# Causal conv and gated FFN on one core: the opening's taps, bands, x cast and first transposes rearranged

## The chip, the cores and the metric

The kernel runs on one core of a Trainium2 chip. The metric is the device time of one execution in microseconds; the time before is the median of three runs. Engines are named as in the profile: PE is TensorE (its weight loads are PEld), DVE is VectorE, ACT is ScalarE, POOL is GpSimd, SP is SyncE, which here issues most transfers.

## The reference

Two stages. First a causal depthwise conv: x is 8 x 4096 x 192, the 192 channels fall into 8 heads of 24, and each head has 7 taps, the softmax of its row of `weight`. Then, on the 32768 x 192 result, a feed-forward stage with 2048 hidden values and the activation h cos(h).

```
w   = softmax(weight, axis=-1)                  # (8, 7)
out[b, s, h, :] = sum_k w[h, k] * x_pad[b, s + k, h, :]    # 6 zero rows ahead of each sequence
h   = out.reshape(32768, 192) @ w_in            # (192, 2048)
y   = (h * cos(h)) @ w_out                      # (2048, 192), float32
```

## The kernel before

**Tiling.** The tokens go in 64 tiles of 512, two to a unit of 1024. For each tile the hidden values come in 8 steps of 256: PE multiplies by w_in into a PSUM tile `h` (`mm1`, L503, a ring of three), ACT takes the cosine (L510), DVE multiplies h by it (L514), and PE multiplies the product by w_out into `o_ps` (`mm2_step`, L552). The conv of later units is made beside this work.

**The conv as a matmul.** A conv over 128 tokens is a matmul with a banded matrix: `band` holds for each head a 128 x 256 matrix, the first half for the tokens' own block and the second for the block behind them. A band consists of four blocks of 32 rows by 38 columns that are alike (E = 38 = 32 + 6). The kernel builds one such block per head and copies it into place. Heads are kept on quarters of the partitions: partitions 32q to 32q + 31 hold the two heads 2q and 2q + 1 (HQ = 2).

**The opening, in program order.** All order is by hand: each engine works off its instructions in the order in which the program gives them.

- ACT issues the load of `weight` into `w_row`, four partitions of 14 values (L81); SP issues the load of the first four blocks of x (L102).
- PE runs zero matmuls that keep its clock up (`keep_warm`, L136). POOL makes `quarter` (L140 to L143), a 4 x 128 matrix of ones in four runs of 32, and one fp32 matmul (L150) spreads the taps to the partitions: `w_bc` is 128 x 14.
- POOL makes `mask` (L158, L159), 32 x 38 x 7, one where tap k of row p falls on column e; ACT and DVE copy it to the other three quarters (L164). POOL then issues the load of w_in (L112), clears a block, and makes the identity (L170).
- Softmax of the taps: maximum and difference on DVE (L176, L178), exponential on ACT (L179), which then loads the table of the sine (L180); sum, reciprocal and product on DVE (L182 to L185) give `wn` in bf16.
- ACT casts the first four blocks of x to bf16 (L398, at L219 in the profile).
- DVE multiplies mask by wn into `prod` (L401, bf16) and sums over the taps into `diag` (L404), 128 x 2 x 38. Behind this sum SP may issue the further loads of x (L406 to L410).
- 16 copies put diag into band (L415): the letters of a string give the engine of each, D for DVE, P for POOL, A for ACT.
- `conv_first` (L426): 32 matmuls in two halves of two blocks each. The result has 64 channels in each of three chunks per block, and each copy (ACT for the first half, DVE for the second, L438) writes them twice side by side into `ct`, since the product with w_in wants every channel on both halves of the partitions. Behind the second copy SP issues the four loads of w_out (L124).
- `turn_first` (L445): for each block three transposes on PE against the identity, 128 columns of ct (a chunk twice) at a time (L453), copied into `cT` by ACT or DVE (L457). Two zero matmuls (one in the second half) stand ahead of them. Then the first tile's products start.

Two strings per tile (`PE_ORDER`, `PE_FIRST`, `ACT_ORDER`, `ACT_FIRST`) give the order of the rest: `h` is a step of mm1, `m` so many steps of mm2, `W` the cast of half of w_out on POOL (L120), `r`, `c`, `d` parts of later convs, `s` a cosine and its product, `p` and `q` marks that the mm2 steps of a tile or half a tile are done.

Of the kernel before, what the change touches and what calls it, by code (L numbers as in the profile page):

```python
# [8 lines left out]
FP32 = mybir.dt.float32  # L9
# [7 lines left out]
def kernel(  # L17
# [8 lines left out]
    nc = tc.nc  # L26
# [52 lines left out]
    HQ = H // 4  # L79
    w_row = consts.tile([4, HQ * K], FP32)  # L80
    nc.scalar.dma_start(out=w_row, in_=weight.rearrange("(q h) k -> q (h k)", q=4))  # L81

# [44 lines left out]

    one = consts.tile([128, 1], FP32)
    nc.vector.memset(one, 1.0)
# [4 lines left out]
    def keep_warm(n, bank=idle):  # L134
        for _ in range(n):
            nc.tensor.matmul(out=bank, lhsT=zero[:, 0:128], rhs=zero, start=True, stop=True)  # L136


    quarter = consts.tile([4, 128], FP32)
    nc.gpsimd.memset(quarter, 1.0)  # L140
    nc.gpsimd.affine_select(out=quarter, in_=quarter, compare_op=ALU.is_ge, fill=0.0, base=0, pattern=[[1, 128]],
                            channel_multiplier=-32)
    nc.gpsimd.affine_select(out=quarter, in_=quarter, compare_op=ALU.is_ge, fill=0.0, base=31, pattern=[[-1, 128]],  # L143
                            channel_multiplier=32)
    scrap = consts.tile([128, 1], FP32)
    nc.scalar.activation(out=scrap, in_=one, func=AF.Exp)
# [3 lines left out]
    nc.tensor.matmul(out=w_all[:, 0 : HQ * K], lhsT=quarter, rhs=w_row, start=True, stop=True)  # L150
    keep_warm(9)

# [25 lines left out]
    nc.vector.tensor_tensor(out=wexp, in0=w_bc, in1=wmax.to_broadcast([128, HQ, K]), op=ALU.subtract)  # L178
    nc.scalar.activation(out=wexp, in_=wexp, func=AF.Exp)  # L179
    nc.scalar.activation(out=scrap, in_=one, func=AF.Sin)  # L180
    wsum = consts.tile([128, HQ, 1], FP32)
    nc.vector.tensor_reduce(out=wsum[:, :, 0], in_=wexp, axis=mybir.AxisListType.X, op=ALU.add)  # L182
# [169 lines left out]
    def taps(u, j, half, mul):  # L352
        if u not in pa:
            pa[u] = pa_pool.tile([128, PA, WN, OR], FP32, name="pa")
        part = slice(HALF * half, HALF * (half + 1))
        mul(pa[u][:, j, part], tap_window(u, j)[:, part], tap[:, j : j + 1])  # L356
# [3 lines left out]
    def conv_raw(u):  # L360

        a, p = pa.pop(u), raw_prod
# [26 lines left out]
    def mend_edges(u):  # L389
# [7 lines left out]

    cast_unit(0, 0, NB, nc.scalar.copy)  # L398

    prod = consts.tile([128, HQ, E, K], BF16)  # L400
    nc.vector.tensor_tensor(out=prod, in0=mask.rearrange("p (o e) k -> p o e k", o=1).to_broadcast([128, HQ, E, K]),  # L401
                            in1=wn.rearrange("p h (o k) -> p h o k", o=1).to_broadcast([128, HQ, E, K]), op=ALU.mult)
    diag = consts.tile([128, HQ, E], FP32)
    summed = nc.vector.tensor_reduce(out=diag, in_=prod, axis=mybir.AxisListType.X, op=ALU.add)  # L404

# [13 lines left out]
    for i in range(2):  # L419
        nc.gpsimd.affine_select(out=pick[:, i, :, :, i, :], in_=pick[:, i, :, :, i, :], compare_op=ALU.not_equal, fill=1.0,  # L420
                                base=0, pattern=[[0, 2], [-32, 4], [0, R]], channel_multiplier=1)
    ct_tiles[0] = ct_pool.tile([128, UB + 1, NC, 2, 64], BF16, name="ct")
    cT[0] = cT_pool.tile([128, NC * (UB + 1) * 128], BF16, name="cT")
    copies = [nc.scalar.copy, nc.vector.tensor_copy]

    def conv_first():  # L426

        banks = o_banks()
        for half in range(2):
            for h in range(H):  # L430
                for prev in range(2):
# [5 lines left out]
                        start=(h == 0 and prev == 0), stop=(h == H - 1 and prev == 1), skip_group_check=True)  # L437
            m = copies[half](out=ct_tiles[0][:, 2 * half : 2 * half + 2].rearrange("p n k t w -> p (n k) t w"),  # L438
                             in_=banks[half][:, 0 : 2 * D].rearrange("p (m t w) -> p m t w", t=1, w=64).to_broadcast(
                                 [128, 2 * NC, 2, 64]))  # L440
        tc.add_manual_dep(nc.sync.nop().ins, m.ins.name, sync_dep, reason="order of the transfers")
# [3 lines left out]
    def turn_first(half):  # L445
        for n in range(2):
# [5 lines left out]
            for k in range(NC):  # L452
                nc.tensor.matmul(out=ps[:, k * 128 : (k + 1) * 128],  # L453
                                 lhsT=ct_tiles[0][:, 2 * half + n, k, :, :].rearrange("p t w -> p (t w)"), rhs=ident,
                                 start=True, stop=True, skip_group_check=True)
            m = NC * (2 * half + n)
# [131 lines left out]

    PE_ORDER = ['m12 h0 m4 h1 K+3 R+1 m5 h2 m7 q h3 U+0 m6 h4 m17 h5 X+1 m9 p h6 h7 O m4', 'm11 h0 m4 h1 m6 h2 m7 q x+1 h3 m5 h4 m7 c1 m8 c2 m3 h5 T+3 L+4 m9 p O h6 h7 m4']
    ACT_ORDER = ['s0 s1 a211 s2 s3 s4 a014 a114 Q s5 P s6 s7 a007', 's0 s1 s2 a102 s3 a203 s4 Q ec2 ec1 s5 P s6 s7']  # L590

    PE_FIRST = ["K1 h0a h0b W0 h1 h2 h3 r h4 w5 d11 w4 h5 d21 W1 c11 X0 m1 h6 m11 h7 L2 c21 D1",
# [5 lines left out]
    ACT_FIRST = ["s0a s0b s1 s2 er s3 s4 ed11 ed21 s5 ec11 s6 ec21 s7",  # L598
                "s0 s1 s2 s3 s4 s5 ec12 ec22 Q P s6 ed12 s7 ed22 ec13 ec23",
                "s0 s1 s2 s3 Q s4 P s5 s6 s7",  # L600
                "s0 s1 s2 s3 s4 ed13 ed23 Q s5 P s6 s7"] + ACT_ORDER

    PE_LAST = "m10 h0 m3 h1 m13 h2 m2 q h3 m10 h4 m3 h5 m7 h6 m12 p h7 O m7"
    ACT_LAST = "s0 s1 s2 s3 s4 s5 s6 P A s7"
# [7 lines left out]
    for t in range(NT + 1):  # L612
        u, second = divmod(t, TPU)
        cu = u + TPU
        if t >= 2 * TPU:
            if second:
                conv["c"] = conv_unit(cu, ring_banks) if cu < NU else iter(())
        pe = PE_LAST if t == NT - 1 else "m%d p" % (2 * STEPS * NT - step) if t == NT else PE_ORDER[second] if t >= len(PE_FIRST) else PE_FIRST[t]
        act = ACT_LAST if t == NT - 1 else ACT_ORDER[second] if t >= len(ACT_FIRST) else ACT_FIRST[t]
# [6 lines left out]
        def flush():  # L626
            while act:
# [3 lines left out]
                else:  # L631
                    need = "p" if k in "PQA" else "h" + k[3:] if k[0] in "ab" else "h" + (k[1:2] if k[2:] in "lr" else k[1:])
                if need not in done:
# [5 lines left out]
                elif k[0] in "ab":  # L639
                    if u + 2 in rT:  # L640
                        taps(u + 2, int(k[1]), int(k[2]), nc.scalar.mul if k[0] == "a" else nc.vector.tensor_scalar_mul)
                elif k[0] == "e":
# [20 lines left out]
        for k in pe.split():  # L663
# [5 lines left out]
            elif k[0] == "m":  # L669
                for q in range(step, step + int(k[1:])):  # L670
                    mm2_step(q)
                step += int(k[1:])
            elif k[0] == "w":
                keep_warm(int(k[1:]), o_pools[0].tile([128, T], FP32, name="o_ps0"))
            elif k == "p":
                assert step % (2 * STEPS) == 0
                made = step // (2 * STEPS) - 1
            elif k == "q":
                assert step % (2 * STEPS) == STEPS
            elif k[0] == "W":  # L680
# [11 lines left out]
            flush()  # L692
            if k == "p" and made == NT - 1:
                finish(NT - 1)
        assert t == NT or not act
# [30 lines left out]
```

## Time and profile before

| | |
|---|---|
| median of 3 runs | 704.99 us (704.95 to 705.27) |
| the profiled execution | 705.18 us, span 703.5 us |
| busy | PE 697.0, ACT 644.4, DVE 642.4, POOL 503.7 us |
| first product with w_in starts | 10.60 us |
| second half of w_out cast | 22.60 us |

The span is that of the engines' work; the execution's own time is 1.7 us longer. Times within the profile count from the span's start. The opening ends about where the second half of w_out has been cast; up to then PE has stretches without work or with zero matmuls, from then on it is busy nearly all the time.

### The profile page before, as it was taken

What the parts mean: (1) busy time and instruction counts of PE and PEld (TensorE: products, weight loads), DVE (VectorE), ACT (ScalarE), POOL (GpSimd) and SP (SyncE); (2) the same over time, 40 slices, a digit from 0 to 9 for tenths busy, and PEclk for the clock granted to TensorE, in tenths of its full rate; (3) what the DMA queues carried; (4) which work ended last, traced back from release to release, by engine and by line L of the source; (5) the groups of instructions that cost most, each with busy time, mean ns of one, the idle gap of its engine ahead of it and who ended that gap; (6) DMA issues with size and microseconds to landing.
All of it is one profiled execution on the core that took longest, in us unless ns stands there. A gap on an engine that the chain in (4) does not pass through costs nothing.

```text
span 703.5 us, 26826 instructions
## 1 busy us (share of the span) xinstructions
PE 697.0 (99%) x11830; PEld 512.8 (73%) x11830; DVE 642.4 (91%) x598; ACT 644.4 (92%) x831; POOL 503.7 (72%) x214
## 2 busy tenths in 40 slices
PE   8999999999999999999999999999999999999997
PEld 4677777777777777777777777777777777777776
DVE  6889999999999999999999999999999999999996
ACT  7889999999999999999999999999999999999875
POOL 6524478977778877778877688877789778799400
PEclk9999999999999999999999999999999999999999
DMA  8964456667667768676656577577665576874331
GB/s 214 234 167 97 120 135 143 138 147 164 138 153 146 131 145 176 134 152 131 147 152 153 150 159 129 140 161 150 143 147 132 145 174 137 153 127 95 92 91 47
DMA packets 228292, 100.09 MB, mean 142 GB/s; under 512 B 156240, under 2 KB 227792, under 8 KB 228176
## 3 DMA queue, kind: packets, MB, share of 16 engines
q1 hardware_dynamic: 227464, 97.40, 62.7%
q8 instruction: 92, 1.51, 0.9%
q0 software_dynamic: 416, 0.79, 0.7%
q14 instruction: 24, 0.20, 0.1%
q10 hardware_dynamic: 296, 0.20, 0.1%
HBM read 31.36 MB, written 25.17 MB: 80 GB/s over the span
## 4 chain that ended last, share of the span: by engine, by line
PE 96%; DMA 1%; DVE 1%; POOL 0%; SPq 0%; ACT 0%; issue 0%; POOLq 0%
PE o_ps L552 48%; PE h L503 46%; PE h L277 2%; DMA wo_f<-in_moe_w_out_dram 1%; PE h L552 0%; SPq L124 0%; PE h L229 0%; DVE band L415 0%; POOL wo L120 0%; POOL mask L159 0%; DVE ct L438 0%; PE o_ps L432 0%; ACT mask L164 0%; DVE diag L404 0%; DVE prod L401 0%
## 5 line engine op out<-in xcount | busy, mean ns | idle before, releaser
L514 DVE TENSOR_TENSOR g<-h,cs 128x1024 bf16<-128x1024 f32 (+1 forms) x513 | 604.9, 1216 | 27.9 <-ACT cs L510 24.5
L510 ACT ACTIVATE cs<-h 128x1024 bf16<-128x1024 f32 (+1 forms) x513 | 511.0, 1021 | 44.0 <-PE h L503 30.6
L552 PEld LDWEIGHTS <-g 64*128 64x128 bf16 x8192 | 354.2, 94 | 102.2 <-issue 1.0
L552 PE MATMUL o_ps<-wo,g 64*128 64x192 bf16 x8128 | 420.6, 243 | 0.1
L503 PE MATMUL h<-cT,w 64*128 64x512 bf16 (+1 forms) x3078 | 407.0, 376 | 0.8 <-DVE g L514 0.4
L503 PEld LDWEIGHTS <-w 64*128 64x128 bf16 x3078 | 147.6, 94 | 75.0 <-issue 1.8
L211 POOL CAST xk<-x_f 128x768 bf16<-128x768 f32 (+1 forms) x56 | 76.4, 1367 | 113.9 <-DMA x_f<-in_x_dram 109.3
L363 POOL TENSOR_TENSOR raw_prod<-rT,tap 128x2784 f32<-128x2784 bf16 x28 | 135.3, 4832 | 0.2
L370 POOL TENSOR_TENSOR raw_prod<-raw_prod,pa 128x2088 f32<-128x2088 f32 x28 | 129.1, 4609 | 2.2
L356 ACT ACTIVATE pa<-rT,tap 128x348 f32<-128x348 bf16 x168 | 94.6, 580 | 0.0
L374 POOL TENSOR_TENSOR raw_prod<-raw_prod 128x1392 f32<-128x1392 f32 x28 | 87.9, 3138 | 2.2
L571 DVE COPY o_sb<-o_ps 128x384 f32<-128x384 f32 x62 | 34.6, 557 | 23.7 <-PE o_ps L552 23.5
L377 POOL TENSOR_TENSOR ro<-raw_prod 128x696 bf16<-128x696 f32 x28 | 46.5, 1660 | 2.2
L294 ACT CAST ct_buf<-h 112x480 bf16<-112x480 f32 x56 | 28.6, 562 | 4.1 <-PE h L277 0.6
L571 ACT COPY o_sb<-o_ps 128x384 f32<-128x384 f32 x64 | 30.8, 482 | 0.1
L277 PE MATMUL h<-xk,band 64*112 64x120 bf16 x448 | 21.2, 213 | 0.0
L277 PEld LDWEIGHTS <-band 64*112 64x112 bf16 x448 | 18.0, 127 | 0.0
L219 POOL CAST x_bf<-x_f 128x768 bf16<-128x768 f32 (+2 forms) x5 | 9.1, 1812 | 7.0 <-DMA x_f<-in_x_dram 6.9
L307 POOL COPY ct<-ct 128x1728 bf16<-128x1728 bf16 x3 | 4.9, 1630 | 8.9 <-ACT ct L239 8.9
L394 POOL COPY cT<-cT 128x144 bf16<-128x144 bf16 x3 | 0.9, 308 | 13.5 <-DMA cT<-ct 13.5
L136 PE MATMUL o_ps<-zero 128*128 128x512 bf16 x21 | 7.2, 492 | 1.3 <-DVE zero L131 1.3
L239 ACT CAST ct<-h 128x432 bf16<-128x432 f32 x12 | 5.9, 530 | 0.4 <-issue 0.4
(66 smaller groups left out, 52.7 us busy)
## 6 DMA issues: line engine op xcount, KB each, us to landing
out_dram<-o_sb SPq DMA_DIRECT2D x63, 384.0 KB, 3.7
x_f<-in_x_dram SPq DMA_DIRECT2D x28, 480.0 KB, 5.5
x_f<-in_x_dram SPq DMA_DIRECT2D x56, 192.0 KB, 2.7
cT<-ro SPq DMA_DIRECT2D x112, 87.0 KB, 2.3
x_f<-in_x_dram SPq DMA_DIRECT2D x4, 384.0 KB, 5.6
wo_f<-in_moe_w_out_dram SPq DMA_DIRECT2D x4, 384.0 KB, 7.9
x_f<-in_x_dram SPq DMA_DIRECT2D x2, 768.0 KB, 5.2
cT<-ct_buf SPq DMA_TRANSPOSE x56, 4.0
```

Of the source, the lines that this page charges most:

```text
L211: copy(out=xk[u][:, NC * n0 : NC * n1].rearrange("p (k n) m -> p k n m", k=NC), in_=x_tiles[u][:, n0:n1].rearrange("p n (m k) -> p k n m", ...
L277: return nc.tensor.matmul(out=ps[h // 4][0:OP, 0 : NPB * 4 * G].rearrange("p (m i r) -> p i m r", m=NC * NPB, i=4)[:, h % 4], lhsT=band[si ...
L356: mul(pa[u][:, j, part], tap_window(u, j)[:, part], tap[:, j : j + 1])
L363: nc.gpsimd.tensor_tensor(out=p, in0=tap_window(u, PA, K), in1=tap[:, PA:K].rearrange("p (j a b) -> p j a b", a=1, b=1).to_broadcast([128, ...
L370: add(out=p[:, 0:m], in0=p[:, 0:m], in1=a[:, done : done + m], op=ALU.add)
L374: add(out=p[:, 0:m], in0=p[:, 0:m], in1=p[:, n - m : n], op=ALU.add)
L377: add(out=ro[u], in0=p[:, 0], in1=p[:, 1], op=ALU.add)
L503: nc.tensor.matmul(out=h[:, i, n0 * 128 : n1 * 128], lhsT=w[rows, k, j, :], rhs=rhs, start=(k == 0), stop=(k == NC - 1))
L510: nc.scalar.activation(out=cs[:, :, part], in_=h[:, :, part], func=AF.Sin, bias=math.pi / 2.0, scale=1.0)
L514: nc.vector.tensor_tensor(out=g_tiles[t][:, 2 * j : 2 * j + 2, part], in0=h[:, :, part], in1=cs[:, :, part], op=ALU.mult)
L552: ms.append(nc.tensor.matmul(out=o_ps[tt, b, si], lhsT=g_tiles[tt][rows, f, s * 128 : (s + 1) * 128], rhs=wo[rows, f // 2, f % 2, :], star ...
L571: (copy or copies[b])(o_sb[t][:, 2 * b : 2 * b + 2, :].rearrange("p s d -> p (s d)"), o_ps.pop((t, b)))
```

## The change

In the opening six things are done in another way:

1. `w_row` lies in one partition, 4 x 14 values. Four fp32 matmuls of 32 columns, with a row of ones as weights, spread it to the four quarters; `quarter` and its three POOL instructions are gone. Seven zero matmuls follow instead of nine.
2. The exponential is one ACT instruction for each of the two heads, and each also writes the head's sum.
3. `prod` is the mask times the exponentials, in fp32; the sum over the taps comes next, and only `diag` is multiplied by the reciprocal of the sums. `wn`, which a later unit needs, is made after the band copies.
4. The first cast of x goes from ACT to POOL (it stands behind the identity, ahead of POOL's band copies).
5. The 16 band copies are six on DVE, six on ACT and four on POOL, instead of 7, 2 and 7.
6. The first conv is copied out once, 384 values a partition instead of 768. The transposes take 64 columns and write 64 partitions, twice for each chunk, 24 in all instead of 12.

The marks `p` and `q` in the order strings are gone, since `m` now finds the end of a tile itself, and the letters of `a` may name a unit. The instructions that come out behind the opening are the same on every engine, in the same order.

```
-    w_row = consts.tile([4, HQ * K], FP32)
-    nc.scalar.dma_start(out=w_row, in_=weight.rearrange("(q h) k -> q (h k)", q=4))
+    w_row = consts.tile([1, 4, HQ * K], FP32)
+    nc.scalar.dma_start(out=w_row, in_=weight.rearrange("(o q h) k -> o q (h k)", o=1, q=4))
...
-    one = consts.tile([128, 1], FP32)
+    one = consts.tile([128, 32], FP32)
...
-    quarter = consts.tile([4, 128], FP32)
-    nc.gpsimd.memset(quarter, 1.0)
-    nc.gpsimd.affine_select(out=quarter, ...)
-    nc.gpsimd.affine_select(out=quarter, ...)
...
-    nc.tensor.matmul(out=w_all[:, 0 : HQ * K], lhsT=quarter, rhs=w_row, start=True, stop=True)
-    keep_warm(9)
+    for q in range(4):
+        nc.tensor.matmul(out=w_all[32 * q : 32 * q + 32, 0 : HQ * K], lhsT=one[0:1], rhs=w_row[:, q], start=True, stop=True)
+    keep_warm(7)
...
-    nc.scalar.activation(out=wexp, in_=wexp, func=AF.Exp)
-    nc.scalar.activation(out=scrap, in_=one, func=AF.Sin)
     wsum = consts.tile([128, HQ, 1], FP32)
-    nc.vector.tensor_reduce(out=wsum[:, :, 0], in_=wexp, axis=mybir.AxisListType.X, op=ALU.add)
-    winv = consts.tile([128, HQ, 1], FP32)
-    nc.vector.reciprocal(winv, wsum)
-    nc.vector.tensor_tensor(out=wn, in0=wexp, in1=winv.to_broadcast([128, HQ, K]), op=ALU.mult)
+    for h in range(HQ):
+        nc.scalar.activation(out=wexp[:, h, :], in_=wexp[:, h, :], func=AF.Exp, accum_out=wsum[:, h, :])
+    nc.scalar.activation(out=scrap, in_=one[:, 0:1], func=AF.Sin)
...
-    cast_unit(0, 0, NB, nc.scalar.copy)
+    cast_unit(0, 0, NB)
-    prod = consts.tile([128, HQ, E, K], BF16)
+    prod = consts.tile([128, HQ, E, K], FP32)
     nc.vector.tensor_tensor(out=prod, in0=mask.rearrange("p (o e) k -> p o e k", o=1).to_broadcast([128, HQ, E, K]),
-                            in1=wn.rearrange("p h (o k) -> p h o k", o=1).to_broadcast([128, HQ, E, K]), op=ALU.mult)
+                            in1=wexp.rearrange("p h (o k) -> p h o k", o=1).to_broadcast([128, HQ, E, K]), op=ALU.mult)
     diag = consts.tile([128, HQ, E], FP32)
-    summed = nc.vector.tensor_reduce(out=diag, in_=prod, axis=mybir.AxisListType.X, op=ALU.add)
+    nc.vector.tensor_reduce(out=diag, in_=prod, axis=mybir.AxisListType.X, op=ALU.add)
+    winv = consts.tile([128, HQ, 1], FP32)
+    nc.vector.reciprocal(winv, wsum)
+    summed = nc.vector.tensor_tensor(out=diag, in0=diag, in1=winv.to_broadcast([128, HQ, E]), op=ALU.mult)
...
-    for i, k in enumerate("DPDPDPDPDPDPDPAA"):
+    for i, k in enumerate("DAPDAPDAPDAPDADA"):
...
+    nc.vector.tensor_tensor(out=wn, in0=wexp, in1=winv.to_broadcast([128, HQ, K]), op=ALU.mult)
...
-            m = copies[half](out=ct_tiles[0][:, 2 * half : 2 * half + 2].rearrange("p n k t w -> p (n k) t w"),
-                             in_=banks[half][:, 0 : 2 * D].rearrange("p (m t w) -> p m t w", t=1, w=64).to_broadcast(
-                                 [128, 2 * NC, 2, 64]))
+            m = copies[half](out=ct_tiles[0][:, 2 * half : 2 * half + 2, :, 0].rearrange("p n k w -> p (n k) w"),
+                             in_=banks[half][:, 0 : 2 * D].rearrange("p (m w) -> p m w", w=64))
...
-                nc.tensor.matmul(out=ps[:, k * 128 : (k + 1) * 128],
-                                 lhsT=ct_tiles[0][:, 2 * half + n, k, :, :].rearrange("p t w -> p (t w)"), rhs=ident,
-                                 start=True, stop=True, skip_group_check=True)
+                for i in range(2):
+                    nc.tensor.matmul(out=ps[64 * i : 64 * i + 64, k * 128 : (k + 1) * 128],
+                                     lhsT=ct_tiles[0][:, 2 * half + n, k, 0, :], rhs=ident,
+                                     start=True, stop=True, skip_group_check=True)
```

More of the change, by code (lines that the diff above doesn't have):

```diff
@@ L136, in keep_warm @@
             nc.tensor.matmul(out=bank, lhsT=zero[:, 0:128], rhs=zero, start=True, stop=True)
-    quarter = consts.tile([4, 128], FP32)
[L140 to L144, printed above, removed]
     scrap = consts.tile([128, 1], FP32)
-    nc.scalar.activation(out=scrap, in_=one, func=AF.Exp)
+    nc.scalar.activation(out=scrap, in_=one[:, 0:1], func=AF.Exp)
     keep_warm(3)
@@ L354, in taps @@
             pa[u] = pa_pool.tile([128, PA, WN, OR], FP32, name="pa")
+        have.add(("tap", u, j, half))
         part = slice(HALF * half, HALF * (half + 1))
@@ L360, in conv_raw @@
     def conv_raw(u):
+        assert {("tap", u, j, half) for j in range(PA) for half in range(2)} <= have
         a, p = pa.pop(u), raw_prod
@@ L617 @@
                 conv["c"] = conv_unit(cu, ring_banks) if cu < NU else iter(())
-        pe = PE_LAST if t == NT - 1 else "m%d p" % (2 * STEPS * NT - step) if t == NT else PE_ORDER[second] if t >= len(PE_FIRST) else PE_FIRST[t]
+        pe = PE_LAST if t == NT - 1 else "m%d" % (2 * STEPS * NT - step) if t == NT else PE_ORDER[second] if t >= len(PE_FIRST) else PE_FIRST[t]
         act = ACT_LAST if t == NT - 1 else ACT_ORDER[second] if t >= len(ACT_FIRST) else ACT_FIRST[t]
@@ L669 @@
             elif k[0] == "m":
-                for q in range(step, step + int(k[1:])):
-                    mm2_step(q)
-                step += int(k[1:])
+                for _ in range(int(k[1:])):
+                    mm2_step(step)
+                    step += 1
+                    if step % (2 * STEPS) == 0:
+                        made = step // (2 * STEPS) - 1
+                        done.add("p")
+                        flush()
+                        if made == NT - 1:
+                            finish(NT - 1)
             elif k[0] == "w":
                 keep_warm(int(k[1:]), o_pools[0].tile([128, T], FP32, name="o_ps0"))
[L675 to L679, printed above, removed]
             elif k[0] == "W":
@@ L692 @@
             flush()
-            if k == "p" and made == NT - 1:
-                finish(NT - 1)
         assert t == NT or not act
```

12 lines of the change are left out of this document (6 added, 6 removed), and 13 rows, old and new, of tables (ACT_FIRST, PE_FIRST).

## The prediction

> **What bounds the kernel now.** I read the page first, its busy shares, then the chain of waits in order of time over the first 26 us, then the timeline of that stretch, and last the DMA by windows.
>
> ```profile
> span 703.5 us, 26826 instructions
> ...
> PE 697.0 (99%) x11830; PEld 512.8 (73%) x11830; DVE 642.4 (91%) x598; ACT 644.4 (92%) x831; POOL 503.7 (72%) x214
> ```
>
> PE is busy for 697.0 of 703.5 us. Only some 6 us exist in which it lacks work, and the kernel's other engines are not the bound. The chain of the opening (start, length, what):
>
> ```profile
> 2.06 0.97 POOL mask L159
> ...
> 3.48 0.41 ACT mask L164
> ...
> 3.91 0.22 ACT wexp L179
> ...
> 4.16 0.18 DVE wsum L182
> ...
> 4.77 0.49 DVE prod L401
> ...
> 5.28 0.72 DVE diag L404
> ...
> 8.19 0.69 PE o_ps L432 x20
> ...
> 8.90 0.97 DVE ct L438
> ...
> 12.16 8.84 DMA wo_f<-in_moe_w_out_dram
> ...
> 21.12 1.48 POOL wo L120
> ...
> 22.64 0.34 PE o_ps L552 x4
> ```
>
> The reader sees one path: mask, softmax of the taps, diagonal, bands, first conv, its copy out; then the transfer of w_out and its cast, and from 22.64 on matmuls. Beside it runs a second path, from the transposes of the first conv to the first product with w_in and the cosines (timeline: start, length, engine, line):
>
> ```profile
> 0.82 0.19 POOL L140 MEMSET quarter<- 4x128 f32 x1 [0.29 <-POOLq L710]
> ...
> 1.67 0.31 POOL L158 MEMSET mask<- 32x266 bf16 x1
> ...
> 2.69 0.20 ACT L146 ACTIVATE scrap<-one 128x1 f32<-128x1 f32 x1
> ...
> 2.70 0.60 PE L150 MATMUL o_ps<-w_row,quarter 4*128 4x14 f32 x2
> 2.98 1.43 POOL L112 DMA_DIRECT2D w<-in_moe_w_in_dram  x2
> ...
> 3.55 0.17 DVE L178 TENSOR_TENSOR wexp<-o_ps,wmax 128x14 f32<-128x14 f32 x1
> ...
> 4.90 0.50 POOL L170 TENSOR_SCALAR_AFFINE_SELECT ident<-ident 128x128 bf16<-128x128 bf16 x1
> ...
> 5.55 1.21 ACT L219 CAST x_bf<-x_f 128x768 bf16<-128x768 f32 x1
> ...
> 6.02 1.86 DVE L415 CAST band<-diag 32x76 bf16<-32x76 f32 x7
> ...
> 6.13 2.00 POOL L415 CAST band<-diag 32x76 bf16<-32x76 f32 x7 [0.73 <-DVE diag L404]
> 6.79 0.51 ACT L415 CAST band<-diag 32x76 bf16<-32x76 f32 x2
> ...
> 8.50 0.80 ACT L438 CAST ct<-o_ps 128x768 bf16<-128x768 f32 x1 [1.20 <-PE o_ps L432]
> ...
> 8.71 0.59 PE L136 MATMUL h<-zero 128*128 128x512 bf16 x2
> ...
> 9.35 0.51 PE L453 MATMUL h<-ident,ct 128*128 128x128 bf16 x6
> ...
> 9.73 1.04 ACT L457 CAST cT<-h 128x384 bf16<-128x384 f32 x2 [0.43 <-PE h L453]
> ...
> 9.90 0.56 DVE L457 CAST cT<-h 128x384 bf16<-128x384 f32 x1
> ...
> 10.60 1.62 PE L503 MATMUL h<-cT,w 64*128 64x256 bf16 x18 [0.18 <-DVE cT L457]
> ...
> 11.14 3.26 ACT L510 ACTIVATE cs<-h 128x512 bf16<-128x512 f32 x4 [0.37 <-PE h L503]
> ```
>
> ```profile
> 22.05 0.93 PE L552 MATMUL o_ps<-wo,g 64*128 64x192 bf16 x12
> ```
>
> Both paths meet in the last row. Its 12 matmuls start at 22.05, and the first 8 take only the first half of w_out; at about 0.04 us each PE would go on at 22.37, but it stands until the second half is cast, 22.64. So w_out ends last, by 0.27 us, and a gain counts only if both paths move: it is the lesser of (gain of the product path + 0.27) and (gain of w_out).
>
> **w_out and the DMA.** The first fence is a window (its length, busy of PE, PEld, DVE, ACT, POOL, granted clock, DMA share, GB/s); the second the POOL queue's share between 6 and 8 us; the third the cast behind the second x load:
>
> ```profile
> 4.00:4.50 0.50, 0.50 (x3) 0.16 (x2) 0.31 (x2) 0.48 (x2) 0.50 (x2) 1.00 0.00 0
> ```
>
> ```profile
> q0 software_dynamic: 143, 0.27, 94.3%
> ```
>
> ```profile
> 11.73 1.23 POOL L219 CAST x_bf<-x_f 128x768 bf16<-128x768 f32 x1 [3.59 <-DMA x_f<-in_x_dram]
> ```
>
> The DMA engines stand empty from 4.0 to 4.5, then w_in, issued by POOL, fills them (94.3% of 6 to 8 us); the later x loads, issued by SP from 6.0 on, and w_out behind them wait for it, and x lands at 11.7. So this train starts with POOL's issue at 2.98, which the change moves. POOL loses the quarter: the mask starts at 0.82 instead of 1.67, 0.85 earlier, and so does the issue behind it (2.13). The train can gain between 0.5 (the empty window alone) and 0.85; I take 0.7, between the two. The issues of x and w_out on SP move with the first band and the ct copy (below, 0.35 later and 0.57 earlier); they do not set the train while w_in still runs. Gain of w_out: 0.7.
>
> **The product path, part by part.**
>
> *Taps in a row.* The earlier mask frees ACT little: its scrap ends at 2.89, then come two mask copies of 0.41, until 3.73 instead of 3.89. The exponential also waits for DVE's subtraction, which ends at 3.72. One fp32 matmul of 128 columns, two passes in 0.60, becomes four of 32 columns, eight passes. No row shows such passes. Low: the first costs 0.30 and each further one a quarter of that, together 0.83, 0.23 more than now. High: each costs 0.30, 1.8 more. I take the low end, the price by columns. The subtraction ends at 3.95, the exponential starts at 3.98 (now 3.91). Two fills fewer behind it cost nothing while bands are awaited (rival below).
>
> *Exponential with sums.* Now 0.25 from its start to the next step. Two of half the length, each writing a sum: low 0.46 (two of 0.22 and a gap), high 0.86 (each followed by a read-out as long as the scrap's 0.20). I take 0.50, near the row of the same operation: prod starts at 4.48. Removed ahead of it are the sum, the reciprocal and wn (4.16 to 4.77).
>
> *Masked sum first.* prod turns from all bf16 to fp32: low as now, 0.49; high, and taken, 0.73, the time of the sum over the same elements with its gap. Then the sum, 0.74 with its gap, the reciprocal, 0.19 (as wsum with its gap), and the product on 76 elements, 0.20 to 0.25. First band copy: 6.37, now 6.02. This part is a loss of 0.35: what is saved ahead of prod is given back by the second exponential, a slower prod and two steps behind the sum. Between all ends it would be 6.1 to 8.3.
>
> *Cast of x by POOL.* ACT loses 1.21, which now holds it until 6.76. POOL's ident ends 0.85 earlier, 4.55, then 1.23 of cast: done at 5.78, under prod and sum. If that cover is gone, POOL's bands and the first conv slip by what it is late.
>
> *Bands.* The slowest now is POOL, seven by 0.286, done at 8.13; the last convs of the first half start at 8.19, 2.17 behind the first band. After: DVE six by 0.266, 1.60; ACT six by 0.255, 1.53; POOL four by 0.286, 1.14. So 1.65 behind: 8.02, a gain of 0.52. wn, 0.2 on DVE, fits between its last band and its ct copy.
>
> *Copied out once.* The ct copies start 0.31 and 0.71 behind that point, at 8.33 and 8.73. They have 384 elements instead of 768, as the cT copies have: ACT 0.49 instead of 0.80, DVE 0.56 instead of 0.97. Ends 8.82 and 9.30. What is late next is PE: its two fills ahead of the transposes start at 8.71 now, 0.52 behind the point, so at 8.54, and hold PE for an estimated 0.45, three quarters of the 0.59 that they take to their end. The transposes start at 8.99, now 9.35.
>
> *Turned twice in column halves.* 12 transposes of 64 columns where there were 6 of 128 (per line: count, shortest, median and longest in ns, first and last start):
>
> ```profile
> L277 PEld LDWEIGHTS <-band x16: 127/127/127, 72.3 to 73.4; 64*112 64x112 bf16 x16
> ...
> L453 PEld LDWEIGHTS <-ct x12: 95/98/98, 9.3 to 10.2; 128*128 128x128 bf16 x12
> L453 PE MATMUL h<-ident,ct x9: 219/219/229, 9.4 to 10.0; 128*128 128x128 bf16 x9
> ```
>
> Now one costs 0.219 and each further 0.058 (six in 0.51). Low: two halves share the array and 12 cost what 6 did, 0.029 each; high: 0.058 each. Weights of 112 columns load slower (127 ns) than those of 128 (98), 16 in about 1.1 us or 0.073 each; by columns 64 cost 0.042, which I take. The twelfth ends at 8.99 + 0.22 + 11 x 0.042 = 9.67, DVE copies it until 10.25 (now 10.46), and the products start at 10.39 instead of 10.60. The page "TensorEngine Tiling" of the Trainium skill, Restrictions and Gotchas, says that column tiling excludes the fast weight load, which speaks against this part; the 127 ns of 112 columns beside 98 of 128 agree. By the weight load in "TensorE: Matmul & The Clock Gate", LDWEIGHTS, 64 columns take an estimated 0.053 us, the products would start at 10.51 and the gain be 0.36.
>
> **Sum.** Product path 0.21: 0.35 lost up to the bands, 0.52 won in them, 0.04 won behind them. ACT's cosines follow the products without a gap (four in 3.26), so PE is ready at 22.16; w_out at 21.94. Gain min(0.21 + 0.27, 0.7) = 0.48. From there on both kernels issue the same instructions, and PE at 99% carries the shift to the end. The profiled run took 705.18 us for its span of 703.5; with 0.48 less, 704.70. Against the median 704.99, 0.19 lower than this run: **704.5**.
>
> **Rivals.**
> - *Nothing moves.* The small matmuls and the sums cost a middle price, the first band slips by another 0.3 to 0.5, and of the 0.27 little is left: 704.8 to 705.2. For: four operations without a row lie on this path. Against: the gain at the bands is plain arithmetic.
> - *POOL's cast and prod collide (slower).* The forecast has prod at 4.48 and the cast at 4.55. If prod comes after 4.55 and must wait for the cast's end, 5.78, the first band slips from 6.37 to 7.69, the products to 11.71, 1.1 later than now, less 0.27 of room: 705.8. Against: now prod (4.77 to 5.26) lies beside POOL's ident (4.90 to 5.40), which took 0.50 for 128 elements where the mask took 0.97 for 266, so it was not held. "SBUF — State Buffer" of the Trainium skill, Who interferes with whom, says that a VectorE instruction with two SBUF inputs contends with a GpSimd instruction that reads SBUF; this overlap shows no blocking.
> - *PE stays slow.* The fills start cold (weight loads of the last two):
>
> ```profile
> 5.77 0.15 PEld L136 LDWEIGHTS <-zero 128*128 128x128 bf16 x1 [0.28 <-issue]
> 6.12 0.10 PEld L136 LDWEIGHTS <-zero 128*128 128x128 bf16 x1 [0.20 <-issue]
> ```
>
>   The wait and load of one are 0.43 at 5.77 and 0.30 at 6.12: the rate doubles near 6. If two fills less delay that past the transposes, the two behind the conv cost 0.43 more and the first products up to 0.5: 705.4. Against: the fills still run until about 6.
> - *More than the sum.* All unknown prices at their low ends: first band 6.1, products near 10.0, a product path 0.64 earlier, and w_out sets the end with 0.85: 704.1.
>
> **How the numbers follow.** Forecast (gain 0.2 to 0.8) 0.55; nothing moves 0.23; collision 0.1; slow PE 0.06; more 0.06. The range, 703.9 to 705.3, runs from the best case to part of the slow ones; the forecast's own is 704.2 to 704.8. 0.2% is 1.41 us, about what a measurement of this kernel tells from no change. Every case lies inside it: a gain above 1.41 needs more than the train's 0.85, a loss above it two unlikely cases at once. So faster 0.05, same 0.91, slower 0.04.
>
> **What would show it.** POOL's issue of w_in near 2.1 and w_out's second cast near 20.4; the first band near 6.4 and all bands 1.65 later; the first product near 10.4; no stand of PE ahead of the first matmul with the second half of w_out. It is wrong if the first band comes after 7, the cast of x takes longer than 1.3, transposes are spaced beyond 0.058, or w_in lands no earlier.

## The result, and the profile after

The changed kernel takes **706.32 us** in the median (705.82 to 707.80), the kernel before, timed beside it, 705.09 us (704.95 to 705.33): a ratio of 1.0019, with a 95% interval of 1.0012 to 1.0026. It is slower by 1.2 us where 0.5 less was forecast. Its single times also lie 2 us apart, those of before 0.4. Fourteen of the sixteen lie between 705.82 and 706.72; the other two, 707.72 and 707.80, have no trace, and what delayed them is open.

The profiled execution took 706.28 us, 1.10 more than that of before; its span is 704.5. In it most steps of the opening came as early as forecast, or earlier (the timeline of the changed kernel, all engines; start, length, engine, line):

```profile
2.06 1.43 POOL L112 DMA_DIRECT2D w<-in_moe_w_in_dram  x2
...
3.68 0.21 ACT L176 ACTIVATE wexp<-wexp 128x7 f32<-128x7 f32 x1
3.80 0.19 ACT L176 ACTIVATION_READ_ACCUMULATOR wexp<-wexp 128x1 f32 x1
...
3.99 0.19 ACT L176 ACTIVATION_READ_ACCUMULATOR wexp<-wexp 128x1 f32 x1
...
4.21 0.71 DVE L395 TENSOR_TENSOR prod<-mask,wexp 128x532 f32<-128x532 bf16 x1 [0.82 <-ACT wexp L176]
4.39 1.59 POOL L211 CAST x_bf<-x_f 128x768 bf16<-128x768 f32 x1
4.95 0.71 DVE L398 TENSOR_REDUCE diag<-prod 128x76 f32<-128x532 f32 x1
...
5.58 0.15 DVE L400 RECIPROCAL winv<-wsum 128x2 f32<-128x2 f32 x1
5.77 0.32 DVE L401 TENSOR_TENSOR diag<-diag,winv 128x76 f32<-128x76 f32 x1
...
6.12 1.61 ACT L412 CAST band<-diag 32x76 bf16<-32x76 f32 x6 [0.43 <-DVE diag L401]
...
8.79 0.56 DVE L436 CAST ct<-o_ps 128x384 bf16<-128x384 f32 x1 [0.99 <-PE o_ps L430]
```

The first band copy starts at 6.12 and the last ends at 7.73 (forecast 6.37 and 8.02). Up to here the change works. PE's own timeline shows where it turns:

```profile
2.64 0.30 PE L145 MATMUL o_ps<-w_row,one 1*32 1x14 f32 x8
2.87 2.33 PE L136 MATMUL o_ps<-zero 128*128 128x512 bf16 x7
6.66 2.09 PE L430 MATMUL o_ps<-x_bf,band 128*128 128x48 bf16 x32 [1.46 <-DVE band L412]
...
9.54 0.85 PE L451 MATMUL h<-ident,ct 128*64 128x128 bf16 x12
...
11.39 0.50 PE L501 MATMUL h<-cT,w 64*128 64x256 bf16 x6
12.12 2.74 PE L501 MATMUL h<-cT,w 64*128 64x256 bf16 x24 [0.23 <-DVE cT L455]
...
20.78 0.26 PE L550 MATMUL o_ps<-wo,g 64*128 64x192 bf16 x2 [0.40 <-POOL wo L120]
...
23.07 0.67 PE L550 MATMUL o_ps<-wo,g 64*128 64x192 bf16 x12
```

PE has no work from 5.20 to 6.66; the transposes, forecast at 8.99, start at 9.54, the products at 11.39 (before 10.60, forecast 10.39), and the twelve matmuls that the prediction put at the end of the opening at 23.07 (before 22.05). The products behind those twelve start at 23.56 instead of 22.81. Times of before read 0.07 more, since its first instruction lies that much further ahead of the rest, so 0.82 of the 1.0 us by which the span is longer is there by then; the rest arises later and is not explained here. The granted clock in the view by windows (PEclk, the third column from the end) says why the stretch between is slow:

```profile
7.00:8.00 1.00, 0.75 (x14) 0.55 (x15) 0.73 (x4) 0.69 (x3) 0.30 (x2) 0.82 1.07 162
8.00:9.00 1.00, 0.78 (x20) 0.70 (x18) 0.20 (x1) 0.48 (x1) 0.00 (x0) 0.50 0.98 154
9.00:10.00 1.00, 1.00 (x11) 0.46 (x12) 0.35 (x1) 0.00 (x0) 0.00 (x0) 0.50 1.03 251
10.00:11.00 1.00, 1.00 (x13) 0.39 (x11) 0.56 (x1) 0.48 (x1) 0.00 (x0) 0.50 1.10 220
11.00:12.00 1.00, 0.89 (x18) 0.50 (x16) 0.50 (x1) 0.55 (x2) 0.00 (x0) 0.98 1.09 325
```

0.82 in the first row and 0.98 in the last put the half clock between 7.64 and 11.04, 3.4 us. Before, these rows read 1.00. The page "TensorE: Matmul & The Clock Gate" of the Trainium skill, Part 1, says that the clock is half or full, by windows of some 3.4 us that run on regardless of the kernel; the 3.4 us agree.

The clock is not all. w_in is issued 0.92 earlier than before, but lands no earlier, which the prediction had named as a sign that it is wrong, and what stands behind it lands later (POOL's timeline; then the last line of the answer for w_in's tile, in us from issue to landing, smallest, median, largest; before 5.5, 6.0 and 6.6):

```profile
12.30 1.23 POOL L211 CAST x_bf<-x_f 128x768 bf16<-128x768 f32 x1 [4.96 <-DMA x_f<-in_x_dram]
...
19.26 1.47 POOL L120 CAST wo<-wo_f 128x1536 bf16<-128x1536 f32 x1 [2.19 <-DMA wo_f<-in_moe_w_out_dram]
21.43 1.47 POOL L120 CAST wo<-wo_f 128x1536 bf16<-128x1536 f32 x1 [0.70 <-DMA wo_f<-in_moe_w_out_dram]
```

```profile
DMA to landing us min/median/max: 6.5/7.4/8.3
```

The second load of w_in (issued at 2.86) lands near 11.2, where before it was 3.78 + 6.6 = 10.4; x is cast at 12.30 instead of 11.73, w_out's halves at 19.26 and 21.43 instead of 17.35 and 21.12.

### The profile page after: what moved, and what is told of

The parts are those of the page before. It is cut to its first block, busy times and chain, and to the rows that moved or that the text cites. A ratio compares the mean times of both kernels' runs of the same rounds, so it can differ in the third digit from the quotient of the medians.

```text
span 704.5 us, 26855 instructions
## 1 busy us (share of the span) xinstructions
PE 696.7 (99%) x11844; PEld 514.1 (73%) x11846; DVE 642.0 (91%) x597; ACT 644.1 (91%) x837; POOL 503.8 (72%) x209
## 4 chain that ended last, share of the span: by engine, by line
PE 97%; DMA 1%; ACT 1%; DVE 0%; POOL 0%; issue 0%; ACTq 0%; SPq 0%; POOLq 0%
PE o_ps L550 48%; PE h L501 47%; PE h L269 2%; DMA wo_f<-in_moe_w_out_dram 1%; PE h L550 0%; PE h L221 0%; ACT band L412 0%; POOL wo L120 0%; ACT L140 0%; PE o_ps L430 0%; ACT mask L159 0%; DVE prod L395 0%; DVE diag L398 0%; DVE ct L436 0%; ACTq L81 0%
## 5 line engine op out<-in xcount | busy, mean ns | idle before, releaser
L211 POOL CAST x_bf<-x_f 128x768 bf16<-128x768 f32 (+2 forms) x6 | 10.7, 1776 | 7.0 <-DMA x_f<-in_x_dram 6.8
```

## The experiments

Three theories stood against each other. **Clock**: with seven fills instead of nine, PE is without work too long, and the clock is at half for part of the opening in some executions. **Transfers**: w_in, issued earlier, runs into x's first load and lands later. **Chain**: the rearranged steps themselves cost more or less than before. All ratios are to the kernel before, timed beside each variant (705.09 to 705.16); they come from all executions and are not the quotients of the medians. Each variant has one trace, so what is said of waits and clocks holds for that execution unless more is said.

### The changed kernel again, without an edit

> The changed kernel once more, unaltered, to see what of its trace is chance. Three theories stand. Clock: the granted clock is halved from 7.6 to 11.0 us since PE has no work from 5.2 to 6.6, and this brings the first product with w_in to 11.4 instead of near 10.3. Transfers: w_in, issued at 2.06 instead of 2.98, runs beside the first x load, and w_out's first half is cast at 19.26 instead of 17.35, so that PE stands 0.4 us for it. Chain: the taps, bands and transposes themselves cost more. Clock and transfers are both put down to the program: the half clock lies within 6.5 to 12 us again, w_out's first cast starts at 19.0 to 19.5, the time is 706.0 to 706.6. If they are chance, either can be missing.

706.24 us, in one execution. This time the clock did not halve: the transposes start at 8.83 and twelve take 0.53. But PE then stands:

```profile
8.83 0.53 PE L451 MATMUL h<-ident,ct 128*64 128x128 bf16 x12
...
11.57 1.47 PE L501 MATMUL h<-cT,w 64*128 64x256 bf16 x17 [1.20 <-DMA w<-in_moe_w_in_dram]
```

The half clock is a matter of chance, the late w_in came again, and each alone delays the products to about the same place. The mean clocks on record for the sixteen timed executions of the changed kernel agree: 3.4 us at half would make 0.998 of the whole, and eight of them read 0.998 or less, eight 0.999 or more, with medians of 706.39 and 706.24 us. The first profile had hidden the second cause behind the first.

### Each cause repaired alone, and both

```
a1   -    keep_warm(7)
     +    keep_warm(12)
a2   -    for t in range(2):            # ahead of the clearing of xb0
     -        load_w(t)
          ... identity ...
     +    for t in range(2):
     +        load_w(t)
a3   both
```

> The changed kernel with 12 zero matmuls instead of 7 behind the spreading of the taps, so that PE has work up to the first conv. Clock theory: no half clock behind 6 us, first product at 10.2 to 10.5; w_out still comes late and PE stands for its first half from about 19.3 to 20.7, so the time falls only to 705.3 to 705.8. Transfer theory alone: as the clock theory here, since the wait for w_out takes what the clock gives. Chain theory: first product still after 11, time 706.0 to 706.6.

705.95 us, ratio 1.0011 (1.0002 to 1.0020). The clock is at full from 7.3 on; until then the fills run at half rate, and the twelve hold the first conv to 7.87. The first product starts at 10.53, and PE then waits 0.47 for w_in. The single times lie 0.84 apart.

> The changed kernel with the load of w_in issued behind the identity on POOL, at about 2.95 us as before the change, nothing else moved. Transfer theory: w_out's first cast starts near 17.4 and its second near 21.1, no stand of PE ahead of the first product with w_out; the half clock stays, so the time is 705.8 to 706.2. If the early w_in is not the cause of the late w_out, its first cast stays at 19.0 to 19.5 and the time at 706.0 to 706.6.

705.87 us, ratio 1.0007 (0.9998 to 1.0016). w_in, issued at 2.77, lands in time, and PE does not wait for it. The single times fall in two groups: four from 705.10 to 705.30, seven from 705.67 to 706.17. The profiled execution (705.87) is of the second. PE's timeline and one row of the windows:

```profile
6.67 2.10 PE L430 MATMUL o_ps<-x_bf,band 128*128 128x48 bf16 x32 [0.62 <-DVE band L412]
8.59 1.03 PE L136 MATMUL h<-zero 128*128 128x512 bf16 x2
9.54 0.85 PE L451 MATMUL h<-ident,ct 128*64 128x128 bf16 x12
```

```profile
8.00:9.00 1.00, 1.00 (x21) 0.70 (x18) 0.20 (x1) 0.48 (x1) 0.00 (x0) 1.00 1.03 178
```

Two fills take 1.03 instead of 0.59 and the twelve transposes 0.85 as under the half clock above, though PEclk reads 1.00. In this execution the clock had not come up at all before about 10.5: the trace's own record of the clock begins there, at 10.47, and the column shows 1.00 ahead of it too. That record begins at 4.22 in the first profile of the changed kernel, at 5.36 in a0 and at 6.03 in the kernel before, each time where a single fill's length turns from 0.63 to 0.38 us, so the place at which the clock comes up differs between executions.

> Both edits. Clock and transfers together: first product at 10.2 to 10.5, w_out's casts near 17.4 and 21.1, then PE waits only for the second half of w_out, and the time is 704.5 to 705.0. Chain theory: above 705.5.

705.11 us, ratio 1.0000 (0.9991 to 1.0009); the single times reach from 704.77 to 705.63. PE's timeline:

```profile
6.96 1.49 PE L430 MATMUL o_ps<-x_bf,band 128*128 128x48 bf16 x32
...
10.09 1.84 PE L501 MATMUL h<-cT,w 64*128 64x256 bf16 x18
...
21.89 0.67 PE L550 MATMUL o_ps<-wo,g 64*128 64x192 bf16 x12
22.39 0.83 PE L501 MATMUL h<-cT,w 64*128 64x512 bf16 x6
```

One repair wins 0.4, both win 1.2: the causes lie side by side ahead of the same products, and the later one sets the time. By the median, both repairs bring the kernel level with the one before, and no further. With both gone, the matmuls behind the twelve start at 22.39 instead of 22.81, and the profiled execution takes 704.89 us, 0.29 less than that of before. So in this execution, one of the faster ones, the chain is worth something, but less than the forecast 0.48: of the 18 matmuls, the second starts only at 10.45, when w_in's second load has landed.

### One part of each cause put into the kernel before

```
b1   w_row in one partition, four matmuls of 32 columns, quarter gone; keep_warm(9) stays
b2   -    keep_warm(9)
     +    keep_warm(7)
```

> The kernel before with one part of the change alone: taps in one row, four small matmuls, the quarter gone; nine fills, bf16 prod, ACT's cast and the double copies stay. Transfers: w_in is issued near 2.1 instead of 2.9, its last packets come after 10.1, x's second half is cast after 12.1 instead of 11.65, and the kernel gets slower although its chain is otherwise untouched: 705.6 to 706.2. Clock: nine fills stay, the clock is up before the first conv, so nothing is lost: 704.9 to 705.2. Chain: the taps are spread in 0.30 instead of 0.60, the first band comes some 0.1 to 0.3 earlier: 704.9 to 705.2.

705.91 us, ratio 1.0013 (1.0004 to 1.0022). This part alone costs 0.75. The products could have started at 10.37; the wait for w_in:

```profile
11.51 1.47 PE L498 MATMUL h<-cT,w 64*128 64x256 bf16 x17 [0.88 <-DMA w<-in_moe_w_in_dram]
```

> The kernel before with seven fills instead of nine and nothing else. Clock: PE has nothing to do from about 6.0 until the first band is there; in some executions the clock is not up, or halves, during the first convs and transposes, so the single times spread over 1 us and the median rises: 705.3 to 706.0. Transfers and Chain: no transfer and no step of the chain is touched, 705.1 with the spread of the kernel before (704.9 to 705.5).

705.32 us, ratio 1.0003 (0.9994 to 1.0012), seven single times from 705.01 to 705.44 and four from 705.86 to 706.27. The profiled execution is one of the latter:

```profile
8.00:9.00 1.00, 0.97 (x25) 0.73 (x24) 0.04 (x1) 0.51 (x1) 0.12 (x1) 0.81 0.98 164
9.00:10.00 1.00, 1.00 (x7) 0.54 (x6) 0.91 (x1) 0.29 (x1) 0.00 (x0) 0.50 1.05 239
```

The median alone is not clear of noise, but the upper group is: none of the 33 executions of the kernel before, timed beside it, is above 705.58. In the profiled one the clock falls from 8.6 on. Two of the four read a mean clock of 0.998, the profiled one among them; the other two read 1.000, and there, without a trace, it stays open whether the clock came up late, as in a2. Seven fills thus cost about 1 us in four executions of eleven, and little in the rest.

### Why an earlier w_in lands later

```
d1   a1, and x's further loads behind the last band copy (7.76) instead of behind the masked sum (6.1)
```

> The changed kernel with twelve fills (w_in issued at 2.06), and x's further loads issued behind the last band copy (near 7.8) instead of behind the masked sum (6.1). Transfers, in the form that the tail of w_in is late since packets of x are between its last ones: with x held back w_in's last packet comes at 9.2 to 9.6 instead of 10.3, PE no longer waits for it at 10.5; x's second half is cast no earlier than 12.2, so the time is 705.5 to 706.3. Rival (w_in lands late since it starts beside the first x load, or since its issue shares something with other engines): its last packet stays after 10.0 and PE still waits 0.3 or more: 705.8 to 706.5.

705.88 us, ratio 1.0010 (1.0001 to 1.0019). Holding x back shortens the wait for w_in from 0.47 to 0.31, but does not end it: w_in's last packet still comes at 10.28 (10.31 in a1). What x gives up here is lost at its own cast. So packets of x between w_in's last ones are at most part of the cause.

```
e1   a3 with keep_warm(10), and load_w between the clearing and the selection of the identity (2.40)
e2   a3 with keep_warm(10) (w_in at 2.77)
f1   b1, and load_w between the clearing and the selection of the identity (2.40)
```

> The changed kernel with ten fills, and w_in issued between the identity's clearing and its selection, near 2.5: halfway between the change's 2.06 and the 2.77 of the late variants. Transfers, in the form that the overlap with x's first load (last packets at 3.8) does the harm: the first packet comes near 4.0, behind x, the last before 9.9, PE does not wait for w_in: 704.8 to 705.1. Rival (each step earlier makes it later, overlap or not): last packet after 10, PE waits for w_in: 705.3 to 705.8. Clock: ten fills last until about 6.3 and leave 0.3 without work; if that is too much, single times above 705.8 turn up.

704.97 us (704.62 to 705.79), ratio 0.9999 (0.9990 to 1.0008). No wait for w_in; the first cosine starts at 10.64 (10.99 in a3, 11.14 before).

> The changed kernel with ten fills, and w_in issued behind the identity, near 2.77, as in the variant with both repairs, which had twelve fills. Clock: if ten fills are enough, 704.8 to 705.1, with the first conv up to 0.3 earlier than 6.96; if not, some of the single times lie above 705.8. Transfers: first packet near 4.3, last near 9.9, no wait for w_in. Chain: w_in is here in time, so the first cosine (10.99 with twelve fills) may come at 10.8: 704.8.

705.13 us (704.79 to 705.91), ratio 1.0001 (0.9993 to 1.0010). The conv starts at 6.69 instead of 6.96, and nothing follows from it: the second product again waits until 10.46. Two of eleven times lie above 705.7, which may be the clock again; no trace shows it, and c1 below, with twelve fills ahead of the conv, has two above 705.9.

> The kernel before with the taps in one row alone, as tried before at 705.91, and nothing else but w_in's issue moved behind the identity's clearing (2.40 instead of 2.06; 2.91 in the kernel before). Transfers, in the form that the overlap with x's first load does the harm: first packet near 3.92, last by 9.7 to 9.9, no wait of PE for w_in, 704.8 to 705.1, at least 0.8 less than with 2.06 from 0.34 of delay. Rival (any issue ahead of 2.9 harms, in proportion): 705.4 to 705.6.

704.99 us (704.77 to 705.46), ratio 0.9998 (0.9989 to 1.0007). Moving one issue by 0.34 takes 0.92 off b1. PE, and then the DMA queues (packets, MB, share; w_in is q0, x is q1), first from 3.0 to 3.9, then from 10 to 12:

```profile
10.38 1.62 PE L498 MATMUL h<-cT,w 64*128 64x256 bf16 x18 [0.18 <-DVE cT L452]
```

```profile
q1 hardware_dynamic: 237, 0.17, 56.2%
...
q1 hardware_dynamic: 947, 0.71, 109.6%
```

The same two stretches of b1, issued at 2.06:

```profile
q1 hardware_dynamic: 300, 0.22, 72.0%
q0 software_dynamic: 9, 0.02, 41.8%
...
q1 hardware_dynamic: 708, 0.53, 103.6%
q0 software_dynamic: 13, 0.02, 5.1%
```

In f1 no packet of w_in is on its way before 3.9, and none is left after 10. In b1 nine start beside x's first load, and thirteen are left. The packets of the variants, worked out from the packets in their traces (us on the scale of the changed kernel's span; the rows of before read 0.07 more):

```
            w_in issued  first packet  95% done  last done  x cast   PE waits for w_in until
before         2.91         4.44         9.69       9.95     11.66    -
a2             2.77         4.27         9.68      10.00     11.65    -
a3             2.77         4.30         9.56       9.94     11.66    10.45
e2             2.77         4.30         9.56      10.06     11.75    10.46
c1             2.77         4.28         9.58      10.23     11.90    10.59
e1             2.40         3.92         9.20       9.68     11.38    -
f1             2.40         3.92         9.24       9.68     11.36    -
e3             2.40         3.94         9.28       9.90     11.58    10.56
after          2.06         3.69         9.74      10.50     12.30    -
a0             2.06         3.63         9.51      10.54     12.62    11.57
a1             2.06         3.64         9.51      10.31     12.23    11.27
b1             2.06         3.66         9.91      10.69     12.53    11.51
d1             2.06         3.57         9.20      10.28     12.47    10.81
```

x's first load does its last packet between 3.73 and 3.88 in all of them. Issued so that its first packet comes just behind that, w_in and x are up to 0.3 earlier than before; issued 0.34 sooner still, w_in's last packet is 0.6 to 1.0 later and x about 1 us, by e1 and f1. That 0.34 of issue time makes the difference is shown by f1 against b1. That it does so by the overlap fits every row of the table, but is not shown apart from the issue time itself: no run moved x's first load and left w_in's issue at 2.06.

How an overlap could do it is not shown either: the trace doesn't say on which DMA engine a packet ran. It does show that a part of the load stays behind: in d1 95% of the packets are done at 9.20, and the rest come one behind the other until 10.28. The traces also keep sixteen completion events for each load. Of w_in's second load nine have come by 9.34 in b1, and the last comes at 11.47; in f1 all sixteen come between 9.05 and 10.01. In d1, with x held back, thirteen have come by 9.28 and the last at 10.77. PE goes on behind the sixteenth, at 11.51 in b1. The last packet is done 0.8 to 1.0 ahead of the end of PE's wait in a0, a1 and b1, and 0.4 to 0.7 ahead of it in the others, d1 among them. The page "DMA: Bandwidth & Descriptors" of the Trainium skill, in "Why a DMA increments its semaphore by 16 and not by 1", says that a load is done only when all 16 engines have reported, each behind its own data; q0's 416 packets, 384 of data and 32 of 4 bytes for two loads, agree with that, and so do the sixteen events. So the load is late because a few of its parts are, not because all of it is slower.

The landing also varies by itself: with the same issue, w_in's sixteenth event comes at 10.05 in e1 and at 10.52 in e3. But in the five traces with the issue at 2.06 it comes from 10.77 to 11.53, in all the others, the kernel before and b2 among them, from 10.01 to 10.60.

### Fewer fills ahead of the transposes

```
c1   a3:   -   keep_warm(2 - half, ps[1])
           +   keep_warm(1 - half, ps[1])
e3   the same edit in e1
```

> Both repairs (twelve fills, w_in issued behind the identity) and, ahead of the first transposes, one fill instead of two and none instead of one. Chain: ACT and DVE have copied the conv out at 8.57 and 9.05, and PE's fills hold the transposes to 8.82 and 9.60; without them the second half's cT copies end about 0.2 earlier than 10.73 and the first cosine starts near 10.8 instead of 10.99: 704.8 to 705.0. Clock: the removed fills let the clock fall again in some executions: spread of 1 us, 705.3 or more. Transfers: w_in (last packet 9.94) then ends the wait for the first product at about 10, so little is won: 705.0 to 705.1.

705.15 us (704.96 to 706.22), ratio 1.0003 (0.9994 to 1.0012). The second half's copies are done 0.2 earlier, and w_in was late again:

```profile
9.91 0.27 PE L501 MATMUL h<-cT,w 64*128 64x256 bf16 x1 [0.26 <-DVE cT L455]
10.59 1.47 PE L501 MATMUL h<-cT,w 64*128 64x256 bf16 x17 [0.41 <-DMA w<-in_moe_w_in_dram]
```

> As the variant with w_in issued near 2.5 and ten fills, with one fill and none instead of two and one ahead of the transposes. Chain: with w_in here by 9.9, the second half's cT copies (10.0 in the variant with fewer fills) let the first cosine start near 10.5: 704.5 to 704.8. Transfers, if w_in lands after 10.2: the products wait for it as they did before (10.59), 705.1 to 705.3. Clock, if the fills were needed: single times above 705.8.

705.31 us (704.61 to 705.56), ratio 1.0001 (0.9992 to 1.0009). Three times of eleven lie below 704.7; in the profiled execution PE waited for w_in until 10.56. A chain ahead of w_in wins nothing. No variant is measurably faster than the kernel before; the lowest median, e1's 704.97, is 0.12 below it, inside its interval.

## Why the prediction was wrong, point by point

**"Gain of w_out: 0.7"** is the step that failed. It took the DMA engines as one pipe that stands empty from 4.0 to 4.5, and let w_in move forward into the time before. The issue came as predicted (2.06 for 2.13), and the bulk of w_in was ahead (the half of the packets at 6.95 instead of 7.52), but the last packets came later, x 0.57 later by the rows, and w_out's second cast at 21.43 instead of 20.4. The prediction's bounds for this gain, 0.5 and 0.85, had no negative end, though no row showed w_in beside x. A gain was there to be had only from the empty window itself: e1 and f1 took 0.3.

**The missing bound.** The prediction used w_in only as the head of a train to w_out. It is also the operand of the first products: before, it lands at 3.78 + 6.6 = 10.4, and the products start at 10.60. With 0.2 of room, any delay of w_in goes straight into them, and the products could not have started at the forecast 10.39 with w_in where it was. That row stood in the trace of before.

**"PE stays slow"**, the rival with 0.06 and 705.4, named the right mechanism and too small a chance. It asked whether two fills fewer delay the first rise of the clock past the transposes, and put 0.43 and 0.5 on that. This is what a2's profile shows, and the size was right for such an execution: the two groups of a2 have medians 0.89 apart. What also happens is that the clock falls again, for 3.4 us. What was wrong is the chance: four executions of eleven (b2) and seven of eleven (a2) are slower by about this much, against the 0.06 that it was given. The four small matmuls that took 0.30 instead of 0.83 made the fills end earlier still, and so did an early rise of the clock: at 5.20 in the first profile, 5.77 in a0 and 6.04 in a2.

**Nothing moves, the collision, more than the sum.** None came true. The cast of x was slower beside prod (1.59, past the 1.3 that the prediction set as its limit, and 1.73 in a3; alone it takes 1.23), but ended at 5.98, ahead of POOL's first band at 6.22, and held nothing. "SBUF — State Buffer" of the Trainium skill, Who interferes with whom, which the prediction weighed and found not to bear out, agrees with this overlap: some 0.4 us longer, hidden here.

**The product path** was better than its terms:
- *Taps in a row*: eight passes took 0.30, not 0.83; the exponential started at 3.68, not 3.98. The price by passes was wrong, and the bounds from 0.83 up excluded the truth.
- *Exponential with sums*: 3.68 to 4.18, 0.50 as predicted; the read-outs overlap the next activation.
- *Masked sum first*: prod 0.74 with its gap, the sum 0.63, the reciprocal 0.19, the last product 0.35 instead of 0.20 to 0.25. First band 6.12 (6.37).
- *Bands*: 1.61 behind the first (1.65).
- *Copied out once*: 0.48 and 0.56 (0.49, 0.56).
- *Turned twice*: at full clock twelve take 0.53 (a0, a3), so (0.53 - 0.22) / 11 = 0.028 each, the low end instead of the 0.042 taken. The rule of "TensorEngine Tiling" of the Trainium skill on the fast weight load, with which the prediction's other price of 0.053 went, does not show in this spacing. It may show in the single load: 64 columns take 110 ns (a3), 128 columns 98 (before). But these loads lie beside one another and beside the matmuls, twelve of them within 0.36. The 127 ns of 112 columns, which the prediction took to agree with the rule, come from matmuls that are not split into column halves, and don't bear on it.

**"ACT's cosines follow the products"** and the sum: in the profiled execution of a3, free of both causes except w_in's landing, the first cosine starts at 10.99, with the span's 0.07 at 11.06, 0.08 ahead of before, and the 0.27 that PE stood ahead of w_out's second half is gone: 0.35 in all, and the matmuls behind that place are 22.81 - 22.39 - 0.07 = 0.35 earlier. a3's median shows nothing of it. The sum had the right form, min(product path + 0.27, w_out), but the product path was bounded by w_in, not by the chain.

**The range** (703.9 to 705.3) held neither: its upper end took in part of a slow PE and no loss on the side of the transfers. The statement that a loss above 1.41 us needs two unlikely cases at once was nearly tested: two happened at once, and since they lie side by side the loss was 1.2.

## What to carry to other kernels

Before an early transfer is issued earlier, look up what it will then run beside, and who needs its last byte: here 0.34 us of issue time, from just behind another load to beside its end, cost 0.9 us, whatever the link between the two. Each load has two deadlines to check, its place in the queue and the first instruction that reads it. Matmuls that keep the clock up are to be counted by the time that they fill, up to the next real work, and where their number changes, several executions have to be timed, since the loss comes by chance.

## What the runs showed of the hardware that was not expected

- A load from POOL's queue whose first packet comes beside the tail of another load ends later than one issued 0.34 us after it (last packet 10.69 and 9.68), though half of it is done at the same time (7.14 and 7.07).
- The granted clock reads 1.00 in stretches where matmuls run at half their rate, ahead of the place where a trace's record of the clock begins (a2: two fills in 1.03 us, the record begins at 10.47).
- Where the clock falls again, it does so 3.41 us after it came up, and for 3.41 us: up at 4.22, down at 7.64, up at 11.05 in the changed kernel's profile; 5.21, 8.62 and 12.03 in b2. PE was without work for part of the stretch ahead of the fall (5.20 to 6.66 in the first).
- An activation with a sum is two instructions, of which the second, the read-out, takes 0.19 us, and lies half beside the next activation.
- Two transposes of 64 columns on the two halves of the array take together what one of 128 takes (0.53 for twelve, 0.51 for six), though a single weight load takes 110 ns for 64 columns and 98 for 128.
- Eight fp32 passes with weights of one row and 32 columns take 0.30 us, half of what two passes of 128 columns took before.
